# Handing out slots of a routed expert layer by waiting tokens: the choice moved to VectorE, the first slot nine steps earlier

## The chip, the core and the metric

The kernel runs on one core of a Trainium2 chip. The metric is the device time of one execution in microseconds (us); a measured time is the median of several executions. TensorE is PE in the rows (its weight loads PEld), VectorE is DVE, ScalarE is ACT, GpSimd is POOL, and SP is the engine whose queue issues most transfers.

## What is computed

Attention over 8 batches of 8 heads (576 positions of width 64) in which each query keeps only its 32 largest scores, and then a layer of 8 experts on the 4608 resulting tokens of width 512. Cut to what matters:

```python
scores = scale * q @ k.T                      # per batch and head, 576 x 576
kth = the 32nd largest score of each row
attn = exp(where(scores >= kth, scores, -1e9) - max); attn /= attn.sum()
x = attn @ v                                  # 4608 tokens of 512
e_idx = argmax(x @ w_gate, axis=1)            # one expert for each token
gate_w = softmax(x @ w_gate)[e_idx]; eom = sigmoid(x @ w_output_gate)
for e in range(8):
    h = relu(x[e_idx == e] @ w1[e])           # 512 -> 1024
    out[e_idx == e] = gate_w * eom[:, e] * (h @ w2[e])
```

## The kernel before

The 4608 queries are 36 tiles of 128, and each tile has four pairs of heads: 144 **steps**. One pass of the main loop (`for i in range(NSTEP + 4)`) does a step in a software pipeline: PE computes scores of a later step (L278), ACT copies them from PSUM (L286), VectorE finds the largest ones (`gmax` L305, `rank` L312 and L315), ACT and POOL mark the rest (`below`: ACT L339, POOL L342, twice each), VectorE reads the marked scores (`window` L354), picks the 32nd (`choose` L365) and sets the others to zero (`weigh` L381, once a head). PE turns the weights (`flip` L408) and multiplies them with v (`attend` L440, in even steps, for two steps at once). A step begins here with the first L312 of `rank`.

When a tile's four steps are done, its rows are scaled, its gate products are made (L470, L479), and a **group** of tiles is **routed** (`group_route`, sixteen small VectorE operations L524 to L570): each token gets a place in a table `ids` in DRAM, region by expert, and POOL scatters the entries (L574). `SORTS` says after which tile a group ends.

An expert's tokens are computed in **slots** of up to 128 rows: `fetch_id`, `fetch_w1`, `fetch_w2` and `fetch_x` load the list, 2 MB of w1, 2 MB of w2 and the rows (POOL gather L704), `turn` (L714) transposes the rows, and four **pieces** do the products: twice `up` (L725, 32 rows of instructions) and twice `down` (L740, 8). One piece stands in each step, from the first step at which a slot is ready, so a slot takes four steps. After the loop the pieces still queued run one after the other, one slot runs its `up` in the same way (`up_plain`), and all further slots take another form (`slots_in_turn`): weights and rows are split in two parts each and multiplied three times (L1048). There are 40 slots in all: 29 handed out after the groups (`EARLY`), 11 (`USUAL`) after the last group; a guarded branch computes more if these don't do.

Which expert and which rows a slot takes is worked out on the chip. Before, `slot_table(g, False)` does it on POOL after each of the nine groups: 34 small operations L602 to L659, queued four at a time behind other work of POOL (`later("ids", ...)`), for slots that have at least a set number of tokens waiting. After the last group the same runs on VectorE (`slot_table(g, True)`).

In the first `LONE` steps (48) no slot is computed. There (`calm`) one head of each pair is finished on ACT and POOL (`veil` L388 and L391, `unveil` L397) and not by VectorE's second L381, and PE fills its odd steps with products of the identity (L922).

Of the kernel before, what the change touches and what calls it, by code (L numbers as in the profile page):

```python
# [10 lines left out]
F32 = mybir.dt.float32  # L11
# [12 lines left out]
P = 128  # L24


SORTS = ((7, 3, 112), (10, 2, 96), (12, 3, 120), (15, 3, 80), (17, 4, 96), (20, 1, 128), (23, 4, 112), (27, 4, 128),
         (31, 5, 64))

USUAL = 11  # L30

# [8 lines left out]
def tile_topk_attention_moe(  # L40
# [47 lines left out]
            else:  # L88
                TT.append(((2 * bp + 1, j - 5),))
    sorts = [x for x in SORTS if x[0] < NTT]  # L90
    ENDS, EARLY, LEAST = zip(*sorts) if sorts else ((), (), ())
    ends = list(ENDS) + [NTT]
    GROUPS = [list(range(a, b)) for a, b in zip([0] + ends, ends)]
    NGRP = len(GROUPS)
# [1 line left out]
    rest = 0  # L96
    for g in range(NGRP - 1):
        rest += len(GROUPS[g]) * P
        rest = min(rest, max(E * (LEAST[g] - 1), rest - EARLY[g] * LEAST[g]))
    rest += len(GROUPS[-1]) * P  # L100
    NLAST = (rest - E) // P + E

# [14 lines left out]
    pads = {nm: consts.tile([1, 8 + E], F32, name="pad_" + nm) for nm in "abcd"}  # L117
    spacer = consts.tile([1, 1], F32, name="spacer")
    first_row = consts.tile([1, E + 1], F32, name="first_row")
    slot_iota = consts.tile([1, MAXS, E], F32, name="slot_iota")  # L120
    slot_off = consts.tile([1, MAXS], F32, name="slot_off")

# [6 lines left out]
    def setup():  # L129

        def iota(x, pattern, base=0, mult=0):
            return lambda: nc.gpsimd.iota(x, pattern=pattern, base=base, channel_multiplier=mult,
                                          allow_small_or_imprecise_dtypes=True)

        def gates():
            for a in range(2):
                for i, w in enumerate((w_gate, w_out_gate)):
                    c0 = a * 16 + i * 8
                    nc.sync.dma_start(
                        wg[a * 64:(a + 1) * 64, :, c0:c0 + E],  # L140
                        w.rearrange("(c a p) e -> a p c e", a=2, p=64)[a])

        at = entry.rearrange("p (b j) o -> p b j o", j=9)
        S2, NBP = 2 * S, NB // 2
        ops = [lambda: nc.gpsimd.memset(wg, 0.0), gates,
               iota(ones, [[1, P]], 0, -1),
               lambda: nc.gpsimd.tensor_scalar(before_b, ones, 0.0, None, op0=ALU.is_gt),
               lambda: nc.gpsimd.memset(ones, 1.0), lambda: nc.gpsimd.memset(ones_b, 1.0),
               iota(first, [[-1, E]], E), iota(carry0, [[REG, E]]),
               lambda: nc.gpsimd.memset(first_row, 0.0),  # L150
               iota(slot_iota, [[1, MAXS], [0, E]], 1), iota(slot_off, [[P, MAXS]]),
               iota(entry[:, :, 0], [[P, NTT]], 0, 1),
               iota(at[:, :, 0:4, 1], [[S2, NBP], [P, 4]], 0, 1),
               iota(at[:, :, 5:9, 1], [[S2, NBP], [P, 4]], S, 1),
               iota(at[:64, :, 4, 1], [[S2, NBP]], 4 * P, 1),
               iota(at[64:, :, 4, 1], [[S2, NBP]], S + 4 * P, 1),
               lambda: nc.gpsimd.memset(entry[:, :, 3], 0)]
        ops += [lambda m=m: nc.gpsimd.memset(m, 0.0) for m in pads.values()]
        return ops
# [28 lines left out]
    def run(exact, stack):  # L188
# [254 lines left out]


        CAR = [carry0]
        done0 = consts.tile([1, E], F32, name="done0")
        nc.gpsimd.memset(done0, 0.0)
        DONE = [done0]
        rows_done = [0]

        def tile_rows(t, g, lg, j):
# [130 lines left out]
        SLOT = {}  # L582
        NEED = []

        def slot_table(g, last):

            n = NLAST if last else EARLY[g]
            least = 1 if last else LEAST[g]
            eng = nc.vector if last else nc.gpsimd
            ops = []  # L590
            add = ops.append
            T = {}
# [1 line left out]
            def tl(name, shape, dt=F32, bufs=1):  # L594
                T[name] = st.tile(shape, dt, name="sl_" + name, bufs=bufs)
                return T[name]
# [2 lines left out]
                T[nm] = pads[nm]  # L599
            def v(name):  # L600
                return T[name][:, 8:]
            add(lambda: eng.tensor_tensor(tl("cnt", [1, E]), CAR[0][0:1], carry0[0:1], op=ALU.subtract))  # L602
            add(lambda: eng.tensor_tensor(tl("wait", [1, E]), T["cnt"], DONE[0], op=ALU.subtract))

            half = (P - least) / P - 0.5 + 0.5 / P
            add(lambda: eng.tensor_scalar(v("a"), T["wait"], 1.0 / P, half, op0=ALU.mult, op1=ALU.add))
# [9 lines left out]
            add(lambda: eng.tensor_scalar(T["past"][:, :n, :], T["past"][:, :n, :], 0.0, 1.0, op0=ALU.max, op1=ALU.min))  # L616

            add(lambda: eng.tensor_scalar(first_row[:, :E], T["d"][:, 7:7 + E], -float(P), None, op0=ALU.mult))
            add(lambda: eng.tensor_tensor(first_row[:, :E], first_row[:, :E], DONE[0], op=ALU.add))
            if last:  # L620
                def count():
                    NEED.append(consts.tile([1, 1], I32, name="need" + tagged))
                    eng.tensor_copy(NEED[0], T["d"][:, 7 + E:8 + E])
                    if not exact:
                        eng.tensor_scalar(over, T["d"][:, 7 + E:8 + E], -float(usual), 0.0, op0=ALU.add, op1=ALU.max)
                add(count)
            add(lambda: eng.tensor_tensor(tl("jump", [1, E]), first_row[:, 1:], first_row[:, :E], op=ALU.subtract))
            add(lambda: eng.tensor_scalar(T["jump"], T["jump"], float(REG), None, op0=ALU.add))

# [11 lines left out]
            add(lambda: eng.tensor_tensor(T["slot"][:, 1, :n], T["way"][:, :n, 0],  # L641
                                          first_row[:, 0:1].to_broadcast([1, n]), op=ALU.add))
            def slots():
                SLOT[g] = (consts.tile([1, 2, MAXS], I32, name="slots" + tagged) if last else
                           st.tile([1, 2, MAXS], I32, name="slots", bufs=3))
                eng.tensor_copy(SLOT[g][:, :, :n], T["slot"][:, :, :n])
            add(slots)
            if not last:

                add(lambda: eng.tensor_scalar(tl("t", [1, E + 1]), T["d"][:, 7:8 + E], -1.0, float(n),  # L650
                                              op0=ALU.mult, op1=ALU.add))
                add(lambda: eng.tensor_scalar(T["t"], T["t"], 0.0, None, op0=ALU.max))
                add(lambda: eng.tensor_tensor(T["t"][:, :E], T["t"][:, :E], T["t"][:, 1:], op=ALU.subtract))
                add(lambda: eng.tensor_scalar(T["t"][:, :E], T["t"][:, :E], float(P), None, op0=ALU.mult))
                add(lambda: eng.tensor_tensor(T["t"][:, :E], T["t"][:, :E], T["wait"], op=ALU.subtract))
                add(lambda: eng.tensor_scalar(T["t"][:, :E], T["t"][:, :E], 0.0, None, op0=ALU.min))
                def dn():
                    d = st.tile([1, E], F32, name="done", bufs=2)
                    eng.tensor_tensor(d, T["cnt"], T["t"][:, :E], op=ALU.add)  # L659
                    DONE[0] = d  # L660
                add(dn)
            return ops


# [96 lines left out]

        NSTEP = NTT * NHP

        LONE = 4 * ENDS[0] + 20 if ENDS else 0

        order = []
        cur = [0]
# [4 lines left out]
        def ahead(what, f, n, after=None, lag=0):  # L772

            while had[what] < min(len(order), cur[0] + n):
                s = had[what]
                if after and when.get((after, s), clock[0]) + lag > clock[0]:
                    return
                f(s, *order[s])
                when[what, s] = clock[0]
                had[what] += 1  # L780
# [24 lines left out]
        def turn_ahead():  # L805
            if had["turn"] < had["x"]:
                evs = []
                ahead("turn", lambda s, *_: evs.append(turn(s, ps_t, "pst")), 1, "x", 2)
                return evs[0] if evs else None

        def heavy_start():
# [52 lines left out]
        def route(g):  # L864
            small.extend(group_route(g, LGT[g]))
            if g < NGRP - 1 and EARLY[g]:
                ops = slot_table(g, False)

                def some(part):
                    for f in part:  # L870
                        f()
                for x in range(0, len(ops), 4):
                    part = ops[x:x + 4]
                    small.append(lambda part=part: later("ids", 0.18 * len(part), lambda: some(part), 3))
                small.append(lambda: not waiting("ids"))
                small.append(lambda: queue_slots(g, EARLY[g], (GROUPS[g][-1] + 1) * P))
                small.append(lambda: step[0] >= known[0] and ids_known())
# [6 lines left out]
        for i in range(NSTEP + 4):  # L884
# [55 lines left out]
                late.append(ev)  # L940
            if 2 <= i < NSTEP + 2:
                (last if calm else late).append(flip(i - 2, 2))
            ev = turn_ahead() if room else None
            if ev:
                late.append(ev)
            for f in early:
                f()
            if i < NSTEP and not calm:
# [10 lines left out]
                fill(1)  # L959
            if 1 <= i <= NSTEP:  # L960
                choose(i - 1)
                fill(4 if calm else 1)
                weigh(i - 1)
            ahead("x", fetch_x, 2, "id", 2)
            run_slow(DMAS, ("ids", "out"))
            if 1 <= i <= NSTEP:
                veil(i - 1)
            for f in last:
                f()
            side_use()  # L970
            fill(4 if calm else 3)
            if i < NSTEP:
                if hp == 0 and t + 2 < NTT:
                    load_q(t + 2)
# [33 lines left out]
        tail[0] = True  # L1008
        HL = {}
        usual = min(NLAST, USUAL)  # L1010
        small_end = lambda: small.extend(slot_table(NGRP - 1, True) + [lambda: queue_slots(NGRP - 1, usual, N)])

        def slots_in_turn():

# [241 lines left out]
```

## Time and profile before

| what | before |
|---|---|
| median of 3 runs | 1271.24 us (1270.17 to 1272.48) |
| profiled execution: its time, its span | 1271.3 us, 1269.5 us |
| PE busy, VectorE busy | 1178.2 us, 1196.9 us |
| ACT busy, POOL busy | 1043.9 us, 759.0 us |
| mean granted PE clock | 0.99 |
| bytes moved | 227.41 MB |

The span runs from the first to the last recorded instruction; 1.8 us of the execution's time lie around it. Busy shares are averages over stages that differ: the first 48 steps have no slots, the loop after them has a piece in each step, and behind the loop there are slots alone. An instruction that waits after it has started counts as busy.

### The profile page before, as it was taken

How to read it: one execution, taken by the hardware profiler on the slowest of the kernel's cores; microseconds unless marked ns; L12 is line 12 of the kernel's file. 1: busy time of each engine (PE TensorE's matmuls, PEld its weight loads, DVE VectorE, ACT ScalarE, POOL GpSimd, SP SyncE). 2: the span in 40 equal slices, each digit the busy share in tenths (PEclk: the TensorE clock that was granted, in tenths of full speed). 3: DMA queues.
4: the chain of work that ended last, by engine and by line, in shares of the span. 5: the costliest groups of instructions: out<-in, count | busy, mean ns of one | idle time of the engine just before them, and what ended most of it. 6: DMA issues, size and time to landing. Idle time of an engine off the chain costs nothing.

```text
span 1269.5 us, 31280 instructions
## 1 busy us (share of the span) xinstructions
PE 1178.2 (93%) x9792; PEld 896.6 (71%) x9792; DVE 1196.9 (94%) x6157; ACT 1043.9 (82%) x1984; POOL 759.0 (60%) x1222
## 2 busy tenths in 40 slices
PE   6888778777699999999999999999999999999997
PEld 5665556555477777777777777777777777788885
DVE  7999999999999999999999999999999984898984
ACT  6999999898888878888888887888888763798884
POOL 6666666698775766757667667567657753132110
PEclk8999999999899999999999999999999999999999
DMA  5400210202818662765464555765554467999982
GB/s 138 77 18 19 71 55 18 56 19 64 290 57 278 202 225 104 249 229 159 174 205 159 211 189 164 258 221 177 207 179 162 151 202 248 373 399 386 379 311 82
DMA packets 109378, 227.41 MB, mean 179 GB/s; under 512 B 14858, under 2 KB 33546, under 8 KB 108176
## 3 DMA queue, kind: packets, MB, share of 16 engines
q1 hardware_dynamic: 99536, 205.67, 48.4%
q0 software_dynamic: 7552, 18.96, 4.3%
q8 instruction: 79, 1.29, 0.5%
q10 hardware_dynamic: 2112, 0.68, 0.3%
q14 instruction: 99, 0.81, 0.2%
HBM read 206.68 MB, written 20.69 MB: 179 GB/s over the span
## 4 chain that ended last, share of the span: by engine, by line
PE 59%; DVE 26%; issue 10%; DMA 2%; POOL 2%; ACT 1%; POOLq 0%; SPq 0%; ACTq 0%
PE pm L725 14%; PE pm L740 13%; PE po L440 10%; PE ps L278 9%; PE pst L408 9%; DVE cand L305 8%; DVE v L354 5%; DVE cand L315 3%; DVE v L312 3%; DVE ep L381 3%; DMA w1t<-in_w_dram 2%; DVE x L365 1%; PE pm L1048 1%; PE pst L461 1%; POOL xg L704 1%
## 5 line engine op out<-in xcount | busy, mean ns | idle before, releaser
L342 POOL TENSOR_TENSOR w<-s,marks 128x576 f32<-128x576 f32 x288 | 362.8, 1281 | 181.4 <-ACT marks L339 170.8
L305 DVE MAX8 cand<-s 128x8 f32<-128x72 f32 x2304 | 322.0, 218 | 8.1 <-ACT s L286 8.1
L408 PE MATMUL pst<-ident,ep 128*128 128x128 f32 x1296 | 206.8, 284 | 55.9 <-ACT ep L397 48.3
L339 ACT ACTIVATE marks<-s,v 128x576 int8<-128x576 f32 x288 | 220.9, 770 | 34.3 <-DVE v L312 30.8
L408 PEld LDWEIGHTS pst<-ident,ep 128*128 128x128 f32 x1296 | 145.8, 142 | 143.6 <-ACT ep L397 59.4
L416 ACT ACTIVATE pT<-pst 128x512 f32<-128x512 f32 (+1 forms) x432 | 197.7, 481 | 7.0 <-PE pst L408 5.2
L354 DVE MAX8 v<-w 128x8 f32<-128x576 f32 x288 | 202.1, 743 | 0.0
L286 ACT ACTIVATE s<-ps 128x1152 f32<-128x1152 f32 (+1 forms) x145 | 162.3, 1120 | 44.9 <-PE ps L278 44.9
L725 PE MATMUL pm<-xs,w1t 128*128 128x128 f32 x1664 | 194.7, 275 | 0.1
L725 PEld LDWEIGHTS pm<-xs,w1t 128*128 128x128 f32 x1664 | 189.9, 192 | 0.3 <-ACT y L747 0.3
L381 DVE SCALAR_TENSOR_TENSOR ep<-s,kth,ep 128x576 f32<-128x576 f32 x240 | 187.9, 812 | 0.3 <-issue 0.3
L278 PE MATMUL ps<-kst,qst 64*128 64x288 f32 (+1 forms) x1280 | 181.0, 431 | 5.4 <-ACT s L286 5.4
L440 PE MATMUL po<-pT,v 128*64 128x128 f32 (+3 forms) x3200 | 185.3, 267 | 0.0
L440 PEld LDWEIGHTS po<-pT,v 128*64 128x64 f32 (+1 forms) x3200 | 157.9, 136 | 33.0 <-issue 31.3
L740 PE MATMUL pm<-w2t,ht 128*128 128x512 f32 x400 | 180.5, 594 | 0.0
L349 ACT ACTIVATE ep<-s,v 128x576 f32<-128x576 f32 x240 | 175.5, 778 | 0.0
L751 POOL DMA_INDIRECT out_dram<-y,idt x40 | 46.6, 1165 | 181.4 <-ACT y L747 164.5
L312 DVE MAX8 v<-cand 128x8 f32<-128x64 f32 x864 | 148.2, 213 | 0.0
L278 PEld LDWEIGHTS ps<-kst,qst 64*128 64x128 f32 (+1 forms) x1280 | 97.7, 177 | 44.2 <-issue 16.1
L740 PEld LDWEIGHTS pm<-w2t,ht 128*128 128x128 f32 x400 | 72.1, 190 | 71.9 <-issue 71.9
L315 DVE MATCH_REPLACE8 cand<-v,cand 128x64 f32<-128x64 f32 x576 | 116.1, 209 | 0.0
L391 POOL TENSOR_TENSOR w<-s,marks 128x576 f32<-128x576 f32 x48 | 61.5, 1280 | 52.0 <-ACT marks L388 51.9
(183 smaller groups left out, 1837.6 us busy)
## 6 DMA issues: line engine op xcount, KB each, us to landing
w1t<-in_w_dram SPq DMA_DIRECT2D x40, 2048.0 KB, 10.0
w2t<-in_w_dram SPq DMA_DIRECT2D x40, 2048.0 KB, 11.9
v<-in_va_dram SPq DMA_DIRECT2D x8, 1152.0 KB, 5.7
x_rows<-xu SPq DMA_DIRECT2D x36, 256.0 KB, 2.6
qst<-in_qa_dram SPq DMA_DIRECT2D x70, 128.0 KB, 10.8
kst<-in_ka_dram SPq DMA_DIRECT2D x14, 576.0 KB, 7.8
ids<-far SPq DMA_DIRECT2D x1, 678.0 KB
xg<-x_rows,idt POOLq DMA_INDIRECT x40, 6.9
```

What stands on the lines that cost most here:

```text
L278: nc.tensor.matmul(ps[qs, a, n, :288], Q[t][rows, hp, qs], K[b][rows, hp, cols], start=True, stop=True)
L305: nc.vector.max(out=c[:, 8 * g:8 * g + 8], in_=SC[i, a][:, g * GW:(g + 1) * GW])
L312: nc.vector.max(out=vs[:, a, 8 * r:8 * r + 8], in_=cs[a])
L339: nc.scalar.activation(m.bitcast(I8).rearrange("p (s b) -> p s b", b=2)[:, :, 1], s, AF.Sign, bias=vs[:, a, PIVOT - 1:PIVOT], scale=-(1.0 ...
L342: nc.gpsimd.tensor_tensor(w, s, m, op=ALU.add)
L354: nc.vector.max(out=VV[i][0][:, a, 24:32], in_=SW[i][0][a])
L381: nc.vector.scalar_tensor_tensor(e, SC.pop((i, a)), kth_col(i, a), e, op0=ALU.is_ge, op1=ALU.mult, accum_out=SM[t][:, 2 * hp + a:2 * hp + ...
L408: nc.tensor.transpose(ps[:, c - c0, :], pt[:, c * P:(c + 1) * P], ident)
L416: nc.scalar.activation(x, ps[:, :n, :], AF.Copy)
L440: nc.tensor.matmul(po[a * 64:(a + 1) * 64, k, qs], lhs, rhs, start=half and not k and not m, stop=(c == 3 and k == 1 and m == len(TT[t]) - 1))
L725: nc.tensor.matmul(ph[:, f - f0, :], w[:, c, f * P:(f + 1) * P], XS[s][:, c, :], start=(c == 0), stop=(c == NC - 1))
L740: nc.tensor.matmul(PY[s], HT[s][:, f, :], w[:, f, :], start=(f == 0), stop=(f == NF - 1))
```

## The change

After each group the slots go to the `n` experts with most waiting tokens (at most 128 count), by ten entries of code on VectorE, eleven instructions, instead of the 34 on POOL. `SORTS` has eleven groups before the last instead of nine: tiles 0 to 3 are a group of their own, with no slot, and the next ends with tile 6 and hands out four. `LONE` is 4*7+12 = 40 instead of 48, and the first piece stands in step 42, not 51. There are again 29 early slots and 11 late ones.

```diff
-SORTS = ((7, 3, 112), (10, 2, 96), (12, 3, 120), (15, 3, 80), (17, 4, 96), (20, 1, 128), (23, 4, 112), (27, 4, 128),
-         (31, 5, 64))
+SORTS = ((4, 0), (7, 4), (10, 3), (13, 3), (15, 1), (17, 5), (22, 3), (24, 2), (27, 3), (30, 2), (32, 3))
...
+        def slot_picks(g):
+            n = EARLY[g]
...
+            add(lambda: nc.vector.tensor_tensor(tl("wait", [1, E]), CAR[0][0:1], place[:, 1, :], op=ALU.subtract))
+            add(lambda: nc.vector.tensor_scalar(T["wait"], T["wait"], float(P), None, op0=ALU.min))
+            add(lambda: nc.vector.scalar_tensor_tensor(tl("key", [1, E]), T["wait"], 2.0 * E, first[0:1], op0=ALU.mult,
+                                                       op1=ALU.add))
+            add(lambda: nc.vector.max(out=tl("top", [1, E]), in_=T["key"]))
+            add(lambda: nc.vector.tensor_tensor(tl("pick", [1, E, E])[:, :n, :],
+                                                T["key"][:, None, :].to_broadcast([1, n, E]),
+                                                T["top"][:, :n, None].to_broadcast([1, n, E]), op=ALU.is_equal))
+            def both():
+                tl("both", [1, 2, E, E])
+                for k in range(2):
+                    nc.vector.tensor_tensor(T["both"][:, k, :n, :], T["pick"][:, :n, :],
+                                            place[:, k, None, :].to_broadcast([1, n, E]), op=ALU.mult)
+            add(both)
+            add(lambda: nc.vector.tensor_reduce(tl("slot", [1, 2, E])[:, :, :n], T["both"][:, :, :n, :], axis=AX.X,
+                                                op=ALU.add))
+            def slots():
+                SLOT[g] = st.tile([1, 2, E], I32, name="slots", bufs=3)
+                nc.vector.tensor_copy(SLOT[g][:, :, :n], T["slot"][:, :, :n])
+            add(slots)
+            add(lambda: nc.vector.scalar_tensor_tensor(T["wait"], T["key"], T["top"][:, n - 1:n], T["wait"], op0=ALU.is_ge,
+                                                       op1=ALU.mult))
+            add(lambda: nc.vector.tensor_tensor(place[:, 1, :], place[:, 1, :], T["wait"], op=ALU.add))
+            return ops
...
-        LONE = 4 * ENDS[0] + 20 if ENDS else 0
+        LONE = 4 * min(t for t, n in sorts if n) + 12 if sorts else 0
...
+                pool, name = (ps_t, "pst") if heavy else (ps_m, "pm")
+                ahead("turn", lambda s, *_: evs.append(turn(s, pool, name)), 1, "x", 2)
...
             if g < NGRP - 1 and EARLY[g]:
-                ops = slot_table(g, False)
...
-                for x in range(0, len(ops), 4):
-                    part = ops[x:x + 4]
-                    small.append(lambda part=part: later("ids", 0.18 * len(part), lambda: some(part), 3))
+                small.extend(slot_picks(g))
...
-            ahead("x", fetch_x, 2, "id", 2)
+            ahead("x", fetch_x, 2, "id", 2 if heavy else 1)
...
-            fill(4 if calm else 3)
+            fill(3)
```

`place` holds expert numbers and, in its second row, how far each expert's region has been handed out. `slot_table` stays for the last group alone, on VectorE; the number of slots it allows for (`NLAST`) is 33 instead of 23, and in calm steps a `fill(4)` became `fill(5)`.

Three places of the order. PE, steps 42 and 43, before: the turns of `flip` (L408), scores (L278), gate products (L470, L461), the filling products (L922) and no product of a slot.

```order
L408 MATMUL pst<-ident,ep 128x128
L278 MATMUL ps<-kst,qst 128x288 x4
L408 MATMUL pst<-ident,ep 128x128 x8
L470 MATMUL pst<-xT,wg 32x128 x4
L461 MATMUL pst<-ident,xT 128x128 x2
L922 MATMUL pm<-ident 128x128 x12
```

PE at the same steps now (line numbers are two higher for these, L747 is `up`, L736 `turn`):

```order
L410 MATMUL pst<-ident,ep 128x128 x5
L747 MATMUL pm<-xs,w1t 128x128 x16
L410 MATMUL pst<-ident,ep 128x128 x4
L736 MATMUL pst<-ident,xg_124 128x128 x4
L280 MATMUL ps<-kst,qst 128x288 x4
L410 MATMUL pst<-ident,ep 128x128 x5
L471 MATMUL pst<-xT,wg 32x128 x4
L462 MATMUL pst<-ident,xT 128x128 x2
L747 MATMUL pm<-xs,w1t 128x128 x16
```

The first `up` piece stands in step 42, behind the turns of an even step, and the second in step 43; the filling products end before.

POOL in step 40 before, where a slot table begins, between the marks of two steps (L342, L391):

```order
L574 DMA ids<-entry,posi 43392x4
L602 TENSOR_TENSOR sl_cnt<-base_3907,carry_73 1x8
L603 TENSOR_TENSOR sl_wait<-sl_cnt,done_121 1x8
L606 TENSOR_SCALAR pad_a<-sl_wait 1x8
L607 TENSOR_SCALAR pad_a<-pad_a 1x8
L391 TENSOR_TENSOR w<-s,marks_81 128x576
L328 TENSOR_SCALAR v_4418<-v_4418 128x2
```

VectorE in step 48 now, where the choice for the third group begins; L314 and L317 are `rank`, L356 `window`, L307 `gmax`, L367 `choose`:

```order
L597 TENSOR_TENSOR sl_wait<-base_5333,place 1x8
L314 MAX v_5419<-cand 128x8 x2
L317 MATCH_REPLACE cand<-v_5419,cand 128x64 x2
L598 TENSOR_SCALAR sl_wait<-sl_wait 1x8
L314 MAX v_5419<-cand 128x8 x2
L600 SCALAR_TENSOR_TENSOR sl_key<-sl_wait,first 1x8
L356 MAX v_5304<-w 128x8 x2
L307 MAX cand<-s 128x8 x16
L602 MAX sl_top<-sl_key 1x8
```

The choice stands one by one between the operations of a step, eight instructions in this step and three in the next; in a calm step five stand in a row.

PE behind the loop, before, from the last product that gives the last group its places (L543) to the first split product (L1048). L181 is the sum of a check that VectorE prepares after the slot table (`unsettled`).

```order
L543 MATMUL pst<-oh_17059,ones_b 128x8
L740 MATMUL pm<-w2t,ht 128x512 x4
L714 MATMUL pst<-ident,xg_124 128x128 x4
L740 MATMUL pm<-w2t,ht 128x512 x4
L181 MATMUL po<-lo,ones 1x2
L725 MATMUL pm<-xs,w1t 128x128 x16
L1027 MATMUL pm<-ident,xg_125 128x128 x4
L725 MATMUL pm<-xs,w1t 128x128 x16
L1048 MATMUL pm<-w1h,xsh 128x512
```

The same now (L762 is `down`, L183 the check, L1064 the split product):

```order
L544 MATMUL pst<-oh_16999,ones_b 128x8
L762 MATMUL pm<-w2t,ht 128x512 x4
L183 MATMUL po<-lo,ones 1x2
L747 MATMUL pm<-xs,w1t 128x128 x16
L1043 MATMUL pm<-ident,xg_124 128x128 x4
L747 MATMUL pm<-xs,w1t 128x128 x16
L1064 MATMUL pm<-w1h,xsh 128x512
```

One `down` and one turn fewer stand between the last group's places and the check, and 12 split slots follow instead of 14.

## Rows read from the trace of the kernel before

**Rows 1.** The page: busy time of each engine (share of the span, instructions), and the granted PE clock in tenths of full speed in 40 slices of the span.

```profile
PE 1178.2 (93%) x9792; PEld 896.6 (71%) x9792; DVE 1196.9 (94%) x6157; ACT 1043.9 (82%) x1984; POOL 759.0 (60%) x1222
...
PEclk8999999999899999999999999999999999999999
```

**Rows 2.** Stretches of the span, by engine: start and end, length, busy us of PE, PEld, DVE, ACT and POOL (instructions), granted clock, DMA share, GB/s. The first is steps 0 to 39, the second runs from step 51 to the end of step 143, the row of 325.20 is steps 48 and 49.

```profile
0.00:269.80 269.80, 211.34 (x2028) 159.70 (x2028) 259.81 (x1616) 244.70 (x518) 183.37 (x259) 0.97 0.23 55
...
347.90:1038.50 690.60, 690.21 (x6074) 516.47 (x6068) 689.00 (x3914) 567.03 (x1155) 458.94 (x786) 1.00 0.57 189
...
325.20:340.80 15.60, 9.05 (x79) 6.83 (x79) 15.35 (x85) 13.03 (x30) 11.83 (x18) 0.85 1.04 395
```

**Rows 3.** PE in order of time (start us, length, line, tiles): the first `up` piece (step 51), a `down` piece (step 93) and the `up` piece of step 143.

```profile
349.52 3.74 PE L725 MATMUL pm<-xs,w1t 128*128 128x128 f32 x32
...
661.31 3.60 PE L740 MATMUL pm<-w2t,ht 128*128 128x512 f32 x8
...
1032.54 3.74 PE L725 MATMUL pm<-xs,w1t 128*128 128x128 f32 x32
```

**Rows 4.** VectorE, ACT and POOL in step 93 and the starts of steps 91 and 95 (first L312); the last line is the group of all L365 by line (busy us, mean ns of one | idle before).

```profile
644.61 0.35 DVE L312 MAX8 v<-cand 128x8 f32<-128x64 f32 x2
...
660.83 1.13 ACT L286 ACTIVATE s<-ps 128x1152 f32<-128x1152 f32 x1 [0.53 <-PE ps L278]
661.85 0.77 ACT L339 ACTIVATE marks<-s,v 128x576 int8<-128x576 f32 x1
...
662.79 2.52 POOL L342 TENSOR_TENSOR w<-s,marks 128x576 f32<-128x576 f32 x2 [1.37 <-ACT marks L339]
...
664.16 1.17 DVE L365 SCALAR_TENSOR_TENSOR x<-left,n,v 128x8 f32<-128x8 f32 x1
...
665.26 0.22 DVE L365 SCALAR_TENSOR_TENSOR x<-left,n,v 128x8 f32<-128x8 f32 x1
...
673.75 0.34 DVE L312 MAX8 v<-cand 128x8 f32<-128x64 f32 x2
...
L365 DVE SCALAR_TENSOR_TENSOR x<-left,n,v 128x8 f32<-128x8 f32 x288 | 79.2, 311 | 0.0
```

**Rows 5.** VectorE at the starts of steps 28, 32, 36, 40, 42, 44, 48, 50 and 51.

```profile
188.19 0.35 DVE L312 MAX8 v<-cand 128x8 f32<-128x64 f32 x2
...
214.06 0.35 DVE L312 MAX8 v<-cand 128x8 f32<-128x64 f32 x2
...
243.94 0.35 DVE L312 MAX8 v<-cand 128x8 f32<-128x64 f32 x2
...
269.80 0.35 DVE L312 MAX8 v<-cand 128x8 f32<-128x64 f32 x2
...
283.17 0.35 DVE L312 MAX8 v<-cand 128x8 f32<-128x64 f32 x2
...
297.34 0.35 DVE L312 MAX8 v<-cand 128x8 f32<-128x64 f32 x2
...
325.19 0.34 DVE L312 MAX8 v<-cand 128x8 f32<-128x64 f32 x2
...
340.77 0.35 DVE L312 MAX8 v<-cand 128x8 f32<-128x64 f32 x2
...
347.87 0.34 DVE L312 MAX8 v<-cand 128x8 f32<-128x64 f32 x2
```

**Rows 6.** PE in step 50, an even step without a piece: the turns behind which a piece would stand.

```profile
344.70 0.76 PE L408 MATMUL pst<-ident,ep 128*128 128x128 f32 x5
```

**Rows 7.** VectorE behind the loop: the first and some later operations that route the last group, and the first ones of its slot table (in brackets: idle before, and what ended it).

```profile
1062.07 0.20 DVE L524 TENSOR_REDUCE mx<-lg 128x5 f32<-128x40 f32 x1
...
1063.50 0.20 DVE L557 TENSOR_REDUCE den<-ex 128x5 f32<-128x40 f32 x1
1063.61 0.19 DVE L560 TENSOR_REDUCE ez<-z 128x5 f32<-128x40 f32 x1
...
1064.40 0.21 DVE L549 TENSOR_TENSOR base<-pst,base 128x48 f32<-128x48 f32 x1 [0.51 <-PE pst L543]
...
1065.24 0.15 DVE L602 TENSOR_TENSOR sl_cnt<-base,carry 1x8 f32<-1x8 f32 x1
1065.42 0.15 DVE L603 TENSOR_TENSOR sl_wait<-sl_cnt,done 1x8 f32<-1x8 f32 x1
```

**Rows 8.** PE behind the loop, and the turns of two split slots eight slots apart (L1027).

```profile
1068.18 3.60 PE L740 MATMUL pm<-w2t,ht 128*128 128x512 f32 x8
1072.78 0.19 PE L181 MATMUL po<-lo,ones 128*1 128x2 f32 x2 [1.00 <-DVE lo L179]
...
1137.37 0.60 PE L1027 MATMUL pm<-ident,xg 128*128 128x128 f32 x4
...
1235.35 0.60 PE L1027 MATMUL pm<-ident,xg 128*128 128x128 f32 x4
```

**Rows 9.** POOL's last scatter of the last group's places, ACT's first split of a slot's weights, and the DMA issues (KB each, median us from issue to landing).

```profile
1070.87 0.97 POOL L574 DMA_INDIRECT ids<-entry,posi  x1 [0.22 <-issue]
...
1074.97 1.91 ACT L1020 ACTIVATE w1h<-w1t 128x2048 fp32r<-128x2048 f32 x1 [2.47 <-DMA w1t<-in_w_dram]
...
w1t<-in_w_dram SPq DMA_DIRECT2D x40, 2048.0 KB, 10.0
...
ids<-entry,posi POOLq DMA_INDIRECT x36, 4.1
```

## What the change was expected to do

> **What bounds the kernel now.** I read the busy times first, then stretches by stage, then the order on each engine inside one four-step period, since a tile repeats every four steps.
>
> PE and VectorE are both near 93 and 94% busy over the whole span [rows 1], so neither alone is the answer. By stage it differs. In the first 40 steps VectorE is busy 259.8 of 269.8 us and PE 211.3 [rows 2]: there every VectorE operation costs its time. From step 51 on both seem full, 690.2 and 689.0 of 690.6 us [rows 2]. PE's share is real: from the `up` piece of step 51 at 349.52 to that of step 143 at 1032.54 lie 92 steps [rows 3] with seven groups routed among them, 7.424 us each or 29.70 for a tile's four. VectorE's share is not: in step 93 the first L365 took 1.17 us where its twin took 0.22, and it ended at 665.33 as POOL's L342 did at 665.31 [rows 4]. What is late there is PE: ACT's copy L286 waited for PE's scores (0.53 us), the marks L339 came after it, POOL waited 1.37 us for them, and VectorE for POOL [rows 4]. Steps 91 to 94 took 673.75 - 644.61 = 29.14 us; without 0.96 of waiting, VectorE's own work is 28.2 per four steps. So in the loop with slots PE sets the pace and VectorE has 29.7 - 28.2 = 1.5 us per four steps to spare. Behind the loop PE alone matters: split slots come 12.25 us apart ((1235.35 - 1137.37)/8) [rows 8].
>
> **The change, part by part.** Slots: pieces begin in step 42 instead of 51, nine steps sooner, so 27 slots instead of 25 are done in the plain form, and 12 instead of 14 are split. Two split slots fewer are worth 2 x 12.25 = -24.5 us. I follow PE from the start to the end for the rest.
>
> *Up to step 40.* VectorE is the bound, so groups cost in full. Quiet steps 28 to 31 took 25.9 us, steps 32 to 35 with the routing of seven tiles 29.9, and steps 44 to 47 with that of three tiles 27.9 [rows 5]: +4.0 and +2.0. The change has a group of four tiles (+2.5, between them) and one of three (+2.0) in place of the seven, and one choice of slots. Its eleven instructions are not in the trace. Nearest are 1x8 operations on VectorE behind the loop: 0.15 us long, and started 0.18 apart where each needs the one before (L602, L603); independent ones start 0.11 apart (L557, L560) [rows 7]. That bounds a choice by 1.2 and 2.1 us. Here five stand in a row: I take 1.7. Step 40 comes at 269.8 - 4.0 + 2.5 + 2.0 + 1.7 = 272.0 instead of 269.8.
>
> *Steps 40 and 41* now do what 48 and 49 did, the passage from calm to the rest: 340.77 - 325.19 = 15.6 us [rows 5], at a PE clock of 0.85 [rows 2]; both versions have this passage, so the clock is in that price. In step 42 the first `up` stands behind the turns, which in step 50 ended 4.7 us after the step's start [rows 5, 6]. First piece: 272.0 + 15.6 + 4.7 = 292.3, where before it was 349.52 [rows 3].
>
> *Step 42 to 143.* 101 steps at PE's 7.424 are 749.8 us: the piece of step 143 starts at 1042.1 instead of 1032.54, +9.6. (Seen from the other side: steps 42 to 50 took 64.7 us without a slot [rows 5] and take 66.8 with one.) Pieces now fall in steps 2, 3, 0, 1 of four, before in 3, 0, 1, 2; the long PE steps are the even ones either way (`attend`), so I price that at nothing, with half a microsecond per ten steps, 5 us, as a bound to either side.
>
> *VectorE's additions in that stretch.* Nine groups are routed there, seven before. Sixteen operations take 65.24 - 62.07 - 0.51 = 2.7 us back to back [rows 7]; between others I take 2.4. With a choice at 1.2 (one by one between a step's operations) a group needs 3.6 us, at 2.1 it needs 4.5. Spare time is 1.5 per four steps, and groups end 8 or 12 steps apart (once 20): 3.0 or 4.5. Four gaps are of 8 steps, 0.6 short each, and some spare time will be lost where the wait is already over: together +4.5, bounds 0 (all hidden) and +14 (at 4.5 us a group, with the loss doubled). If the cover were gone altogether, the eleven instructions alone would be 10 to 19 us.
>
> The Trainium skill, "VectorE: DVE Perf Modes", section "The DRAIN you can't avoid", says that the next operation does not start until the pipe of the one before has emptied. L560 started 0.11 us after L557, which took 0.20 [rows 7], so the row shows less than that for independent operations. By the rule each instruction would cost its own length and a choice about 2 us everywhere; the sum would end about 5 us later, near 1266, which lies in the third rival below.
>
> *POOL* loses the 34 slot operations a group. In the loop POOL waits for ACT [rows 4], so this gives nothing there.
>
> *Behind the loop* one `down` piece (3.6 us [rows 8]) and one turn fewer stand ahead of L181. But L181 already waited 1.00 us for VectorE (L179), which comes behind the slot table [rows 8]. The 3.6 becomes wait there: nothing gained. The table grows from 23 to 33 slots; at 1x184 against 1x264 I price that under 0.3. The first slot of the last group is now second in line, not fourth: its list waits on ACT's queue, ahead of the first weight split, until the last scatter has landed: about 4.1 us after its start [rows 9], which would be 1075 in the clock of before and earlier with four tiles instead of five. The split ran at 1074.97 [rows 9], held by its weights. So nothing here; bound +5 if ACT is held by one more landing.
>
> Sum: +9.6 + 4.5 - 24.5 = -10.4 us. The profiled execution took 1271.3 (span 1269.5 and 1.8 around it; the median is 1271.24), so 1260.9, say 1261.
>
> **The rivals.** *VectorE keeps its waits and becomes the bound.* The waits at L365 sum to about 79.2 - 288 x 0.22 = 16 us [rows 4]. They depend on where in a step PE stands; if they stay while group work is added, VectorE needs 101/4 x 28.2 = 712 us, 9 x 4.5 = 40 and 16: 768 against PE's 750, so +18 instead of +4.5: 1274, slower than before. It decides once VectorE's total passes PE's by about 17 us. For it: 712 + 9 x 3.6 = 744 already comes close to 750. Against it: a late VectorE lets PE catch up, and it is PE's lateness that makes the wait.
>
> The Trainium skill, "SBUF — State Buffer", section "Who interferes with whom", states that a VectorE instruction with two SBUF inputs blocks against a GpSimd one that reads SBUF. The ends of L365 and L342 agree with it [rows 4]. Seven of the eleven instructions are of that kind, but none stands between `gmax` and L365, where L342 runs.
>
> *Everything hides.* VectorE's spare time takes all group work, and the passage at steps 40, 41 is a few us shorter since POOL has no slot table: 1261 - 4.5 - 3 = 1253.5.
>
> *The gain is given back in part*: a slot's data late at step 42 (w1 lands 10 us after its issue [rows 9], and the issue stands about three steps ahead), group work at its upper bound, or ACT held behind the loop: +5 to +10, 1266 to 1271.
>
> *The change doesn't do what it says*: if the fuller choice left more than 11 slots for the end, the guarded branch would add over 12.25 us each. Counted from the reference's own tokens, what is left needs 11 in both versions. I give it none.
>
> **How the numbers follow.** Forecast (1257 to 1265) 0.5; everything hides 0.2; given back in part 0.2; VectorE the bound 0.1. Below and above these tails I leave 2 in 10: range 1252 to 1270. Within 0.2% (2.5 us) of 1271.2 is about what a measurement of this kernel can tell from no change. Faster than 1268.7: 0.5 + 0.2 + half of the third case = 0.8; the same 0.1; slower 0.1.
>
> **What would show it.** After: first `up` piece near 292; PE's pieces again 29.7 us per four steps, with PE waiting for VectorE only in group steps; the first L365 near 0.2 us in steps 48, 49 and their like; 12 split slots 12.25 apart; L183's wait for VectorE near 5 us. Wrong would be the pace: above 30.2 per four steps over the loop, VectorE is the bound; or a first piece after 300.

## The result, and the profile after

The changed kernel takes 1278.92 us (median, 1276.83 to 1280.82) where the kernel before took 1271.27 on the same chip: 1.0058 times as long, 95% interval 1.0044 to 1.0073. On another chip the ratio was 1.0036 (1.0022 to 1.0051). It is slower; I had forecast 1261 and a range of 1252 to 1270. The profiled execution has a span of 1277.1 us.

The page of the changed kernel (busy time, share, instructions; granted PE clock in 40 slices), which answers [rows 1]:

```profile
PE 1179.8 (92%) x9770; PEld 892.7 (70%) x9770; DVE 1195.2 (94%) x6293; ACT 1023.4 (80%) x1960; POOL 662.6 (52%) x929
...
PEclk8999999999999999999999999999999999899999
```

POOL lost its 34 operations a group (759.0 to 662.6 us), and PE and VectorE are as busy as before. The page doesn't show what went wrong. The places that the sum went through do. VectorE at the starts of steps 40, 42 and 143 (its first L314 there), and PE in the first `up` piece and in that of step 143, which answer [rows 3, 5]:

```profile
274.94 0.35 DVE L314 MAX8 v<-cand 128x8 f32<-128x64 f32 x2
...
288.96 0.21 DVE L314 MAX8 v<-cand 128x8 f32<-128x64 f32 x1
...
293.51 3.74 PE L747 MATMUL pm<-xs,w1t 128*128 128x128 f32 x32
...
1058.71 0.22 DVE L314 MAX8 v<-cand 128x8 f32<-128x64 f32 x1
...
1060.80 3.74 PE L747 MATMUL pm<-xs,w1t 128*128 128x128 f32 x32
```

| us | before | forecast | after | after against forecast |
|---|---|---|---|---|
| step 40 starts | 269.80 | 272.0 | 274.94 | +2.9 |
| first piece | 349.52 | 292.3 | 293.51 | +1.2 |
| from it to the piece of step 143 | (another count of steps) | 749.8 + 4.5 = 754.3 | 767.3 | +13.0 |
| from there to the end of the span | 237.0 | 212.5 | 216.3 | +3.8 |

The three lower lines add up to the whole miss of 18.0 us. The forecast column is the prediction's own sum, with the span 1.8 us under the time.

So 13 of the 18 us lie in the loop with slots. PE's waits name them: engine, line, what it waited for, total us, times, longest.

```profile
PE pm L736 <- ACT y L769: 13.1, 11, 1.4
...
PE po L183 <- DVE lo L181: 5.3, 1, 5.3
...
PE pm L1064 <- DVE w1l L1037: 1.8, 1, 1.8
```

L736 is `turn`, which stood in no wait of PE before. Eleven of its 28 runs wait for L769, ScalarE's copy of the finished slot's result. One of them, in time order (PE, ACT and VectorE in VectorE's step 49; in brackets the idle time before, and what ended it):

```profile
347.61 0.74 ACT L418 ACTIVATE pT<-pst 128x512 f32<-128x512 f32 x2
...
348.24 0.66 PE L410 MATMUL pst<-ident,ep 128*128 128x128 f32 x4 [0.24 <-ACT pT L418]
348.25 1.43 ACT L351 ACTIVATE ep<-s,v 128x576 f32<-128x576 f32 x2
...
349.58 0.68 ACT L769 ACTIVATE y<-pm,idt 128x512 f32<-128x512 f32 x1
349.59 0.20 DVE L367 SCALAR_TENSOR_TENSOR x<-left,n,v 128x8 f32<-128x8 f32 x1
...
350.31 0.66 PE L736 MATMUL pm<-ident,xg 128*128 128x128 f32 x4 [1.41 <-ACT y L769]
```

The turn writes `pm`. There is one `pm` bank, and the slot's last `down` piece has just left its result in it. ScalarE empties it, but only after two copies of weights (L418) and two exponentials (L351) that stand ahead in its queue. PE has only the four L410 to do in between and stands still for 1.41 us. VectorE's L367 took 0.20 us there, as I had forecast for L365: VectorE does not wait for POOL in this step, and it is PE that falls behind. Two lines of the change put the turn there: the one that chooses between `pst` and `pm`, and one that is not in the diff's core above:

```diff
...
-            ev = turn_ahead() if room else None
+            ev = turn_ahead() if room or not heavy else None
...
```

`heavy` holds the pieces still to come. In the step that takes out the last piece it is empty, so a turn made there goes to `pm`. A turn has `room` in a `pst` bank only while no gate product is pending, in steps 1 and 2 of a tile, and in step 1 alone where a group is routed. Before, every turn went to `pst`, and a slot's last piece fell in step 2: by the new rule, too, a turn in step 1 would still have had a piece behind it. Now the last piece falls in step 1, and a turn there goes to `pm`: the phase that I had priced at nothing, together with the new choice of the bank.

The trace also has what speaks for the rival that VectorE became the bound. The chain that ended last, by engine, before (first line) and after:

```profile
PE 59%; DVE 26%; issue 10%; DMA 2%; POOL 2%; ACT 1%; POOLq 0%; SPq 0%; ACTq 0%
```

```profile
DVE 63%; PE 18%; issue 12%; ACT 4%; POOL 2%; DMA 0%; POOLq 0%; ACTq 0%
```

It went from PE to VectorE. The prediction's own sign says the same: from step 42 to 143 four steps take 30.5 us, above the 30.2 at which VectorE was to be the bound. The two readings ask for different repairs, so they were set against each other.

### The profile page after: what moved, and what is told of

Read it like the earlier page. It is cut to its first block, busy times and chain, and to the rows that moved or that the text cites. A ratio compares the mean times of both kernels' runs of the same rounds, so it can differ in the third digit from the quotient of the medians.

```text
span 1277.1 us, 31052 instructions
## 1 busy us (share of the span) xinstructions
PE 1179.8 (92%) x9770; PEld 892.7 (70%) x9770; DVE 1195.2 (94%) x6293; ACT 1023.4 (80%) x1960; POOL 662.6 (52%) x929
## 4 chain that ended last, share of the span: by engine, by line
DVE 63%; PE 18%; issue 12%; ACT 4%; POOL 2%; DMA 0%; POOLq 0%; ACTq 0%
DVE cand L307 19%; DVE v L356 11%; DVE ep L383 10%; DVE cand L317 7%; DVE v L314 6%; PE pm L747 6%; DVE x L367 4%; PE po L442 3%; PE ps L280 3%; PE pm L762 2%; PE pst L410 2%; ACT ep L351 1%; POOL xg L726 1%; ACT marks L341 1%; DVE lg L499 1%
## 5 line engine op out<-in xcount | busy, mean ns | idle before, releaser
L344 POOL TENSOR_TENSOR w<-s,marks 128x576 f32<-128x576 f32 x288 | 363.4, 1283 | 243.8 <-ACT marks L341 240.2
L307 DVE MAX8 cand<-s 128x8 f32<-128x72 f32 x2304 | 322.0, 217 | 16.0 <-ACT s L288 16.0
L410 PE MATMUL pst<-ident,ep 128*128 128x128 f32 x1296 | 205.6, 284 | 47.3 <-ACT ep L399 39.5
L410 PEld LDWEIGHTS pst<-ident,ep 128*128 128x128 f32 x1296 | 145.4, 141 | 135.9 <-ACT ep L399 48.4
L418 ACT ACTIVATE pT<-pst 128x512 f32<-128x512 f32 (+1 forms) x432 | 197.2, 482 | 48.6 <-PE pst L410 46.5
L747 PE MATMUL pm<-xs,w1t 128*128 128x128 f32 x1792 | 212.8, 278 | 0.0
L747 PEld LDWEIGHTS pm<-xs,w1t 128*128 128x128 f32 x1792 | 207.1, 194 | 0.2 <-issue 0.2
L356 DVE MAX8 v<-w 128x8 f32<-128x576 f32 x288 | 202.0, 742 | 0.0
L762 PE MATMUL pm<-w2t,ht 128*128 128x512 f32 x432 | 194.4, 593 | 0.0
L383 DVE SCALAR_TENSOR_TENSOR ep<-s,kth,ep 128x576 f32<-128x576 f32 x248 | 193.6, 810 | 0.6 <-PE pm L747 0.3
L351 ACT ACTIVATE ep<-s,v 128x576 f32<-128x576 f32 x248 | 180.8, 778 | 0.0
L314 DVE MAX8 v<-cand 128x8 f32<-128x64 f32 x864 | 147.6, 211 | 0.0
L762 PEld LDWEIGHTS pm<-w2t,ht 128*128 128x128 f32 x432 | 77.9, 190 | 77.5 <-issue 77.5
L773 POOL DMA_INDIRECT out_dram<-y,idt x40 | 49.3, 1233 | 145.0 <-ACT y L769 131.4
L317 DVE MATCH_REPLACE8 cand<-v,cand 128x64 f32<-128x64 f32 x576 | 116.0, 209 | 0.0
L330 POOL TENSOR_SCALAR v<-v 128x2 f32<-128x2 f32 x144 | 32.0, 222 | 126.5 <-DVE v L314 124.8
```

What stands on the lines that cost most here:

```text
L307: nc.vector.max(out=c[:, 8 * g:8 * g + 8], in_=SC[i, a][:, g * GW:(g + 1) * GW])
L314: nc.vector.max(out=vs[:, a, 8 * r:8 * r + 8], in_=cs[a])
L317: nc.vector.match_replace(out=cs[a], in_to_replace=vs[:, a, 8 * r:8 * r + 8], in_values=cs[a], imm_value=LOW)
L344: nc.gpsimd.tensor_tensor(w, s, m, op=ALU.add)
L356: nc.vector.max(out=VV[i][0][:, a, 24:32], in_=SW[i][0][a])
L383: nc.vector.scalar_tensor_tensor(e, SC.pop((i, a)), kth_col(i, a), e, op0=ALU.is_ge, op1=ALU.mult, accum_out=SM[t][:, 2 * hp + a:2 * hp + ...
```

## The experiments

**e1: the turn to the other bank.** Nothing but the bank changes; the turns stay where they are.

```diff
...
-                pool, name = (ps_t, "pst") if heavy else (ps_m, "pm")
+                pool, name = (ps_t, "pst") if room else (ps_m, "pm")
...
```

> The turn that stands in the step of a slot's last piece goes to a pst bank, as the other turns do, wherever there is room (ten of eleven cases), instead of the one pm bank that the piece's own result still holds. Theory (PE's eleven waits in L736 for ScalarE's L769, 13.1 us, are the loss): 1278.9 - 13 = about 1266, the loop's pace from step 42 to 143 falls from 7.62 to about 7.49 us a step and the long steps of 8.8 us go. Rival (VectorE's group work sets the pace and PE only waits inside its slack): 1276 or more, the pace stays near 7.62.

Measured: 1262.61 us, 0.9914 of the kernel before (0.9897 to 0.9931). The wait is left once, at a turn without room:

```profile
PE pm L736 <- ACT y L769: 1.0, 1, 1.0
```

VectorE at the starts of steps 42 and 143 in e1:

```profile
288.35 0.21 DVE L314 MAX8 v<-cand 128x8 f32<-128x64 f32 x1
...
1043.89 0.22 DVE L314 MAX8 v<-cand 128x8 f32<-128x64 f32 x1
```

That is 755.5 us between them instead of 769.7: 14.2 less, for 12.1 less of waiting. Of the loop's steps over 8.5 us nine become one. One bank turns a loss of 0.4 to 0.6% into a gain of 0.9%.

**e2: the phase undone.** The first piece is held back to step 43.

```diff
-            if heavy or when.get(("turn", s), clock[0]) >= clock[0]:
+            if heavy or step[0] < 43 or when.get(("turn", s), clock[0]) >= clock[0]:
```

> The first piece stands one step later (step 43), so pieces fall in steps 3, 0, 1, 2 of four as in the kernel before, and every turn but one finds a pst bank while a piece of the slot before is still to come; all else as changed. Theory: the waits of L736 go (-13), one piece more is left behind the loop, where PE waited 5.3 us at L183 anyway: 1266 to 1269.5. Rival (VectorE's group work): 1279 to 1283.

Measured: 1261.06 us, 0.9905 (0.9888 to 0.9923), better than expected. The rule on banks is that of the changed kernel, yet only one turn meets a full `pm`; the loop takes 753.1 us. Starting one step later is faster than starting sooner.

```profile
PE pm L736 <- ACT y L769: 0.5, 1, 0.5
```

VectorE at the starts of steps 42 and 143 in e2:

```profile
286.84 0.21 DVE L314 MAX8 v<-cand 128x8 f32<-128x64 f32 x1
...
1039.94 0.23 DVE L314 MAX8 v<-cand 128x8 f32<-128x64 f32 x1
```

**e4: the same bank, the copy sooner.** The turn stays in `pm`; the copy of the last piece goes ahead of the exponentials.

```diff
-                late.append(ev)
+                (late if heavy else early).append(ev)
```

> The turn stays in pm; instead ScalarE copies a slot's result (L769) ahead of the step's two exponentials (L351), not behind them. Theory: the wait of L736 for L769 shrinks from 1.4 to under 0.5 us a time, some 9 to 13 us in all, and at most a few us come back through the later exponentials: 1266 to 1273. Rival (VectorE's group work): 1277 to 1281.

Measured: 1268.24 us, 0.9958 (0.9943 to 0.9972), as the theory expected. The wait shrinks from 13.1 to 1.3 us, and the loop from 769.7 to 760.8. A third way of taking the wait away gives a gain too, smaller than e1's by 5.6 us, which fits exponentials that now start later; that part was not tried by itself.

```profile
PE pm L736 <- ACT y L769: 1.3, 4, 0.3
```

**e8: the wait multiplied.** In e2, every turn is held back to the last piece.

```diff
-            ev = turn_ahead() if room or not heavy else None
+            ev = turn_ahead() if not heavy else None
```

> As e2, but every turn is held back to the step of the slot's last piece and goes to the pm bank: 25 more turns behind the copy L769 than in e2, 14 more than in the changed kernel. Theory (each such turn costs PE its wait, about 1.2 us, and PE sets the pace): 1261 + 25 x 1.2 = 1291, with a wait of L736 for L769 of about 30 us. Rival (the waits lie in PE's slack): 1261 to 1270 in spite of a wait of 30 us.

Measured: 1271.09 us, 0.9985 (0.9973 to 0.9998). The expected size was wrong: a wait is mostly 0.34 us here, not 1.2.

```profile
PE pm L736 <- ACT y L769: 10.8, 26, 1.2
```

VectorE at the starts of steps 42 and 143 in e8:

```profile
287.17 0.22 DVE L314 MAX8 v<-cand 128x8 f32<-128x64 f32 x1
...
1051.24 0.22 DVE L314 MAX8 v<-cand 128x8 f32<-128x64 f32 x1
```

One of the waits in time order:

```profile
354.23 0.66 PE L736 MATMUL pm<-ident,xg 128*128 128x128 f32 x4 [0.34 <-ACT y L769]
```

The last piece falls in step 2 here, behind `attend`, and ScalarE has finished more of its queue by the piece's end. But the price of a microsecond of wait can be read: 10.3 us more wait than e2, 10.0 us more time (on another chip; profile against profile the loop takes 764.1 against 753.1). Within about a microsecond, the wait costs its whole length.

**e3: VectorE's part priced.** In e1, each choice of slots is made a second time into scratch tiles.

```diff
+                small.extend(slot_again(g))
                 small.extend(slot_picks(g))
```

> As e1, with the eleven instructions of every choice of slots a second time into scratch tiles. Theory (PE sets the pace, VectorE has slack between groups): 1 to 8 us above e1. Rival (VectorE is the bound): ten times 1.4 to 1.7 us, 14 to 17 above e1.

Measured: 1271.66 us, 0.9984 (0.9973 to 0.9995), 9.05 above e1: a little over the theory's range and far under the rival's. By the trace 2.9 us of it come before step 42, from one choice in the calm steps, and 6.3 from nine choices in the loop, where steps 42 to 143 take 761.9 against 755.5. That is 0.7 a choice, and the eleven instructions are 2.1 us long in the mean: about a third of VectorE's additional work is exposed there. VectorE is near the bound but is not it. Steps 42 and 143 of e3:

```profile
291.30 0.22 DVE L314 MAX8 v<-cand 128x8 f32<-128x64 f32 x1
...
1053.15 0.22 DVE L314 MAX8 v<-cand 128x8 f32<-128x64 f32 x1
```

**e5: the new choice without the earlier start.** e2 with the first slot where it was before.

```diff
-        LONE = 4 * min(t for t, n in sorts if n) + 12 if sorts else 0
+        LONE = 4 * min(t for t, n in sorts if n) + 20 if sorts else 0
```

with `step[0] < 51` in place of 43.

> As e2 with the first slot eight steps later (LONE 48, first piece in step 51 as in the kernel before): the new choice and the eleven groups without the earlier start. By the sum two more slots are split (2 x 12.25 = +24.5), steps 43 to 50 are without a piece (-2.1), and the last group's first slot stands further back, so that its gather is not waited for (-3): 1261 + 19 = about 1280, some 7 us slower than the kernel before on this chip. Rival (the earlier start gives little, the new choice gives the gain): 1270 or less.

Measured: 1278.44 us, 1.0044 (1.0031 to 1.0056). The choice on VectorE and the eleven groups, with the change's smaller edits, cost 0.4% without the earlier start; the start eight steps sooner is worth 1278.4 - 1261.1 = 17.4 us (expected 19). The rival falls: the gain is all in the start.

**e6: nine groups.** e2 with two groups fewer, again 29 early slots and 11 late ones.

```diff
-SORTS = ((4, 0), (7, 4), (10, 3), (13, 3), (15, 1), (17, 5), (22, 3), (24, 2), (27, 3), (30, 2), (32, 3))
+SORTS = ((4, 0), (7, 6), (12, 3), (13, 2), (17, 6), (23, 5), (26, 2), (30, 4), (32, 1))
```

> As e2 with eight groups that hand out slots and the group of tiles 0 to 3 ahead of them, nine in place of eleven, again 29 early slots and 11 late ones. The second choice in e3 cost 0.9 us a time of about 1.7 of its own work; if VectorE's group work is exposed by half, two groups of some 4 us fewer give 4 us: 1257. If it is hidden (PE the bound): 1260 to 1261. If it is wholly exposed: 1253.

Measured: 1259.48 us, 0.9888 (0.9873 to 0.9904): the lowest of all, but its interval overlaps e2's, and the loop takes 753.1 us in both profiles, so nothing of the two groups is seen there. Whether they save anything elsewhere stays open.

**e7: 30 early slots.** e2 with eleven other groups, 30 slots early and 10 late.

```diff
+SORTS = ((4, 0), (7, 6), (12, 2), (13, 3), (16, 1), (18, 1), (19, 4), (22, 2), (24, 3), (27, 4), (32, 4))
...
-USUAL = 11
+USUAL = 10
```

> As e2 with 30 early slots and 10 late ones from other groups, eleven of them again. The last group's first slot is then third in line behind the loop, not second. If the 3.1 us in which the split turn (L1043) waits for that slot's gather come from its place in line, they go: 1258. If the gather is late for another reason, 1261.

Measured: 1260.19 us, 0.9894 (0.9878 to 0.9909), too close to e2 to be told from it. The part behind the loop tells more. PE at the second split slot's turn (L1043), first in e2, then in e7:

```profile
1098.92 0.63 PE L1043 MATMUL pm<-ident,xg 128*128 128x128 f32 x4 [3.10 <-DMA xg<-x_rows,idt]
```

```profile
1099.31 0.60 PE L1043 MATMUL pm<-ident,xg 128*128 128x128 f32 x4
```

The 3.10 us wait for the gather of the last group's first slot is gone, as it is in e5, where that slot also stands further back. That fits its place in line as the cause, but the wait isn't there every time: the first profile of the changed kernel has none, and that of e9, the same kernel, has 2.90 us. From the start of step 143 to the end the kernel before takes 239.0 us, e2 217.9 and e7 214.9: -24.0, nearly the -24.5 of the sum.

**e9: the changed kernel again.**

> The changed kernel once more, on the chip of e8, so that its ratio to the kernel before stands beside the others: 1.0058 as before, within its interval.

Measured: 1278.61 us, 1.0036 (1.0022 to 1.0051). The expected 1.0058 lies outside, but the intervals overlap: slower by 0.4 to 0.6%. The wait of L736 is 13.2 us in 11 times. Behind the loop the same kernel went another way; PE there:

```profile
1102.39 0.19 PE L183 MATMUL po<-lo,ones 128*1 128x2 f32 x2 [5.31 <-DVE lo L181]
...
1102.51 5.25 PE L747 MATMUL pm<-xs,w1t 128*128 128x128 f32 x32
...
1120.12 0.63 PE L1043 MATMUL pm<-ident,xg 128*128 128x128 f32 x4 [2.90 <-DMA xg<-x_rows,idt]
```

## Why the prediction was wrong, point by point

**The step that failed** is "Pieces now fall in steps 2, 3, 0, 1 of four, before in 3, 0, 1, 2; the long PE steps are the even ones either way (`attend`), so I price that at nothing", with 5 us as its bound. I asked what the shift does to the length of PE's steps. I didn't ask what else is tied to those steps: the turn, which finds a `pst` bank only in steps 1 and 2. The line of the diff that sends it to `pm` was in view, and I gave it no price; with one `pm` bank and ScalarE's queue from the trace it could have been worked out. It measured 13.1 us. The shift taken back (e2) or the bank changed (e1) gives 1261.1 and 1262.6, or 0.9905 and 0.9914 of the kernel before, where the forecast was 0.992.

The Trainium skill, "Perfetto Trace Analysis", section "Matmuls", says that independent groups of matrix products should go round different PSUM banks, so that one is emptied while the next is computed. It is the rule that spoke against this edit, and I did not weigh it. e1 agrees with it: another bank, and 12.1 of 13.1 us of waiting are gone.

**PE's pace of 7.424 us** held: 101 steps at it are 749.8, and steps 42 to 143 took 753.1 in e2 and 755.5 in e1.

**VectorE's additions** at +4.5 (0 to 14): the loop took 3.3 in e2 and 5.7 in e1 beyond PE's own, which is the size forecast; that these microseconds are VectorE's is not shown, and e6's loop is no shorter with two groups fewer. The size of a choice was too small where nothing hides it. VectorE in step 36 of the changed kernel, a calm step, and in step 37:

```profile
252.16 0.14 DVE L597 TENSOR_TENSOR sl_wait<-base,place 1x8 f32<-1x8 f32 x1
252.34 0.16 DVE L598 TENSOR_SCALAR sl_wait<-sl_wait 1x8 f32<-1x8 f32 x1
...
252.91 0.18 DVE L603 TENSOR_TENSOR sl_pick<-sl_key,sl_top 1x32 f32<-1x32 f32 x1
254.37 0.75 DVE L609 TENSOR_TENSOR sl_both<-sl_pick,place 1x32 f32<-1x32 f32 x2
255.15 0.21 DVE L612 TENSOR_REDUCE sl_slot<-sl_both 1x8 f32<-1x64 f32 x1
...
260.78 0.15 DVE L616 CAST slots<-sl_slot 1x8 int32<-1x8 f32 x1
```

The first ones start 0.18 apart as assumed, but the two L609 take 0.75 us together. All L609 of the kernel (shortest, median and longest in ns), and POOL beside the two:

```profile
L609 DVE TENSOR_TENSOR sl_both<-sl_pick,place x20: 146/164/646, 254.4 to 1011.1; 1x24 f32<-1x24 f32 x10, 1x16 f32<-1x16 f32 x4, 1x32 f32<-1x32 f32 x2, 1x8 f32<-1x8 f32 x2
...
253.33 1.64 POOL L393 TENSOR_TENSOR w<-s,marks 128x576 f32<-128x576 f32 x1 [0.21 <-issue]
```

The first of the two took 0.646 us and ended at 255.01, just after POOL's L393 (254.97). In nine of the ten choices one instruction took 0.60 to 0.65 us, and each ended 0.02 to 0.04 us after an instruction of POOL (L393 here, L484 in the loop). That fits the blocking which the prediction set aside because none of the eleven stands where L342 runs: POOL's other instructions would do it too. No run tests it by itself, and four of the nine are L616, a copy with one input, which the prediction didn't count among the seven. Steps 36 to 39 are 28.3 us long, 2.4 over the 25.9 of a quiet four, where I took 1.7 and a bound of 2.1; without the long L609 they would be some 0.5 us shorter (an estimate, 0.646 less the median of 0.164). With groups at 3.2 (steps 20 to 23, and again 32 to 35) instead of 2.5 and 2.0, step 40 came 2.9 late; the passage took 14.0 instead of 15.6, and 1.2 were left at the first piece.

Of the rule on the DRAIN in the Trainium skill ("VectorE: DVE Perf Modes", section "The DRAIN you can't avoid"), which I had set aside: by it a choice costs about 2 us everywhere, an estimate. In the calm the 2.4, less the 0.5 of the long L609, lie between it and my 1.7 and decide nothing; in the loop e3 exposes 0.7.

**The rival "VectorE is the bound"** is out as the cause, though the chain of waits ran through VectorE for 63%, the pace passed the prediction's sign for it, and its price of 1274 lies nearest the time measured. That nearness is chance: with the group work left as it is, e1 and e2 come back to the forecast. In e1, which is 16 us faster than the changed kernel, the chain is still

```profile
DVE 73%; PE 11%; issue 11%; POOL 2%; DMA 2%; ACT 1%; POOLq 0%; ACTq 0%
```

I take it that two engines which wait on each other in each step share the chain by fractions of a microsecond. What tells them apart is the price of additional work: a microsecond for each on PE (e8), a third on VectorE (e3). That the waits in L365 would stay while group work is added did not come true: L365 took 79.2 us in all before [rows 4], and as L367 it takes 69.2 in e1:

```profile
L367 DVE SCALAR_TENSOR_TENSOR x<-left,n,v 128x8 f32<-128x8 f32 x288 | 69.2, 276 | 0.0
```

**Behind the loop** twelve split slots stand 12.25 apart from the third on, as forecast, and L183 waits 5.3 us, as forecast. Two costs were missing. The first is the clock after that wait. PE in time order in the changed kernel, which answers [rows 8]:

```profile
1100.96 0.19 PE L183 MATMUL po<-lo,ones 128*1 128x2 f32 x2 [5.32 <-DVE lo L181]
1101.08 6.45 PE L747 MATMUL pm<-xs,w1t 128*128 128x128 f32 x32
```

Stretches of the same kernel (columns as in [rows 2]; the granted clock stands behind POOL's): the wait, the two behind it, and a later one.

```profile
1095.70:1100.90 5.20, 0.00 (x0) 0.00 (x0) 4.89 (x20) 0.66 (x1) 3.26 (x6) 0.89 1.03 395
1101.10:1104.30 3.20, 3.20 (x17) 3.20 (x16) 0.58 (x4) 0.00 (x0) 0.00 (x0) 0.50 0.90 191
1104.30:1107.50 3.20, 3.20 (x21) 3.20 (x21) 1.00 (x1) 1.91 (x1) 0.00 (x0) 0.64 0.84 313
1107.80:1111.50 3.70, 3.70 (x35) 3.70 (x34) 3.21 (x4) 2.65 (x3) 1.04 (x1) 1.00 0.05 16
```

The same piece in e2, behind a wait of 1.21 us:

```profile
1082.24 0.19 PE L183 MATMUL po<-lo,ones 128*1 128x2 f32 x2 [1.21 <-DVE lo L181]
1082.36 3.84 PE L747 MATMUL pm<-xs,w1t 128*128 128x128 f32 x32
```

At 0.50, the lower level of 1.2 GHz, the piece takes 6.45 us instead of 3.84. "The 3.6 becomes wait there: nothing gained" was thus 2.6 too kind here, and 1.4 in e9, where the piece took 5.25. The second is the place in line of the last group's first slot, which I had priced at nothing with a bound of 5: 3.1 us in e2. In this profile of the changed kernel a split of weights (L1037, 1.8 us) is waited for instead, and in e9's the gather, 2.90 us. Together, 2.6 and 1.8, they are a little over the 3.8 us by which that part missed.

**What stays open.** e1 is 16 us faster than the changed kernel (1278.6 on e8's chip), and the waits taken away are 12.1. Profile against profile the spans differ by 13.6; the profiled execution of e1 was the slowest of its six (1265.28 us). In the loop the profiles differ by 14.2, so 2 us more than the waits; these were not traced to a place.

## What to carry to other kernels

When a change shifts work by a step, list everything that is tied to those steps (banks, room for side products, the queue of the engine that empties a bank) and not the lengths of the steps alone; an operation sent to the only bank whose content was still being copied out waited here, up to 1.41 us, for all that stood ahead in the copy engine's queue. With two engines both near 94% busy, the chain of waits didn't say which was the bound; adding a known amount of work to each did. Of the kernels here, the earlier start with the turn in a free bank or the pieces one step later (e1, e2, e6) beats both the kernel before, by 0.9 to 1.1%, and the changed one.

## What the hardware showed that was not expected

A wait of PE can have two prices, its length and the clock behind it. The 1.41 us waits at L736 left the granted clock at 1.00. VectorE's steps 49, 50 and 51, with the wait in the first (columns as in [rows 2]):

```profile
343.80:351.30 7.50, 5.85 (x27) 3.13 (x27) 7.50 (x43) 6.10 (x12) 4.25 (x7) 1.00 0.00 1
351.30:358.30 7.00, 7.00 (x82) 6.22 (x79) 7.00 (x43) 5.30 (x11) 5.11 (x8) 1.00 0.72 239
358.30:367.10 8.80, 8.80 (x97) 7.21 (x97) 8.08 (x45) 7.63 (x16) 4.48 (x7) 1.00 0.92 351
```

The step from 358.3 is the long one of 8.8 us: PE, late by its wait, is busy throughout, and now VectorE is the one that waits (8.08 of 8.80). The wait of 5.32 us at L183 was followed by a clock of 0.50, and so cost half as much again (2.6 us). The second price isn't the same each time: behind the same wait in e9 it was 1.4 us. In e2 the gather's wait of 3.10 us was followed by 0.64 (first line), in e9 that of 2.90 us by 1.00 (second line). What decides between them no run here shows.

```profile
1098.90:1102.00 3.10, 3.08 (x11) 2.51 (x12) 0.69 (x1) 2.42 (x3) 0.15 (x2) 0.64 0.94 260
```

```profile
1120.10:1123.20 3.10, 3.08 (x16) 2.62 (x17) 0.69 (x1) 2.42 (x3) 1.09 (x2) 1.00 0.90 269
```
